# Attention and mixture of experts on one core: the stray lists emptied one by one, fewer late rows zeroed, and a new order of the steps

## Chip, cores and metric

One core of a Trainium2 chip runs the program. The metric is the device time of one execution in microseconds (us). Several executions of the kernel are timed and their median is taken; one more is profiled, and its rows are the ones shown here.

## What is computed

Attention over 8 batches with 8 heads, 576 tokens and 64 dimensions, whose keys and values are first condensed into 32 memory slots by a softmax of `phi` over the tokens, and then a top-1 mixture of 8 experts on the 4,608 tokens of 512 features that the attention gives:

```python
a = softmax(phi, axis=2)                        # 8 x 8 x 576 x 32
k_m = einsum('bhsm,bhsd->bhmd', a, k)
v_m = einsum('bhsm,bhsd->bhmd', a, v)
attn = softmax(q @ k_m.transpose(0, 1, 3, 2) / 8)
x = (attn @ v_m).transpose(0, 2, 1, 3).reshape(4608, 512)
logits = x @ w_gate                             # 512 x 8
expert_idx = argmax(logits, axis=1)
gate_w = softmax(logits)[arange(4608), expert_idx]
for e in range(8):
    mask = expert_idx == e
    h = maximum(x[mask] @ w1[e], 0)             # 512 x 1024
    out[mask] = gate_w[mask, None] * (h @ w2[e])   # 1024 x 512
```

## The kernel before

**Batches and strays.** The eight batches run one after the other, with the attention of the next batch woven into the expert work of the present one. Most tokens of a batch go to the same expert. The kernel finds that expert (step R6, `largest`; for batch 0 a guess), reads its number into SP's register (`expert_id`, L670, the TENSOR_LOAD of `ei`) and loads only its weights: w1 in four chunks of 512 KB into tiles wraw (step LW, `load_w1`, L614; batch 0 by halves, L621), w2 in four more (steps D0 to D3, `load_w2`, L631). All tokens of the batch run through this expert. Tokens that belong to another expert, the strays, are listed: GpSimd scatters one entry of 16 bytes for each token into one of five lists in DRAM, `stray_list` 0 to 4, one for each tile of 128 tokens (steps Y0 to Y4, `send_stray`, L600; a token that is no stray has a position out of bounds and writes nothing). After the last batch, `stray_slot` reads the first 32 entries (step entries, L816), gathers their attention rows from the DRAM tile `ad` (fetch, L845), runs them through their expert and scatters the rows out. The rows of strays of the last batch, which is not yet stored then, go through the DRAM tile `late` instead (L922); `fetch_late` (L730) reads rows of tiles 3 and 4 of it, and `done` (L751) adds them to that batch's output.

**What must be filled first.** A list must hold BIG wherever no entry is written, and `late` must hold zeros. The tile `empty` (128 x 336 words) is set to BIG at the start (L222). Step CE (`empty_lists`, L229 to L231) writes it into all five lists, 336 KB each. Step CY (`empty_late`, L224 to L227) clears a tile `zero`, which it takes from the pool of the output tiles (tag "y", two buffers), and writes it over all 576 rows of `late`, 1,152 KB.

**One batch.** A softmax of phi (A, A1, B, C), kvm (E, `memory`, L310: 144 small matmuls on TensorE), keys pk and values pv (G, V: L336, L347) with their copies kb and vT by ScalarE (L341, L351), scores sT (J, L441), a softmax of them and its transpose eT (K to M3), which is split into a high and a low part (S, T: eh by ScalarE, el by VectorE). A matmul of the full precision is made of three fp32r products of high and low parts. pu = V x W1 (U0, U1: L377, 16 records for each half) is split into uh by ScalarE and ul by VectorE (L381, L384). The steps i make ph (L698), 16 of them in a batch; the steps e split relu(ph) into hh and ht by ScalarE (L639) and hl, ht by VectorE (L642). The w2 chunks are split by W0 to W3: whi by ScalarE (L608), wlo by GpSimd (L609) in most batches. The steps o make py (L743, and L651 for the last, short tile), 20 parts of a batch; y0 to y4 (`done`, L756, L661, L667) scale and store the tiles (L724, 64 KB each). R to R4 make the logits, the one-hot choice and the histogram; X to X6 the gates and the positions of strays; N (L430) stores the attention rows into `ad`.

**What sets the order.** The table ORDER lists every step of the kernel once, as a batch digit and the step's name (`1LW` is LW of batch 1; `1o03` is tile 0, part 3 of its output). The program runs the steps in that order and chains the instructions of each engine in it (end of `tile_memory_attention_moe_kernel`), so each engine's queue holds them as the table lists them. SP issues nearly all DMAs, GpSimd the scatters and gathers. The DMAs of SP use eight semaphores in turn, so that a DMA also waits for the one eight places ahead of it.

```python
yp = ctx.enter_context(tc.tile_pool(name="yp", bufs=2))
late = dram.tile([S, DM], F32, name="late")
ld_list = [dram.tile([LIST, 4], F32, name="stray_list%d" % i) for i in range(NT)]
```

Of the kernel before, what the change touches and what calls it, by code (L numbers as in the profile page):

```python
# [9 lines left out]
F32 = mybir.dt.float32  # L10
# [22 lines left out]
1LW 21Q 2A2 1X4 0y3 1X 20B 21B 1T1 21C 1D0 0o12 0o13 0y1 11N 1X1 1X2 0o21 0o22 1U0 1UH10 1UH00 20Q 1UL10
1UL00 20C 0o42 0o43 0y4 0z 1D2 1D1 3LQ 0o23 0y2 1U1 1UH01 1UL01 0X2 0X5 10N 1X5 1i00 1i01 1UH11 1UL11 0X6 0Y0
2E 2D 1e01 1e00 1i03 1e03 2FV 20F 21F 1i02 1e02 1i13 1e13 2V 1i05 2G 2G1 1W0 2V1 1i17 1e17 1W1 2J 21K
20K1 1e05 2V2 1i04 1e04 20K 1W2 00N 1i06 1e06 0Y3 0Y2 1i16 1e16 1i07 1e07 21K1 3L1 21K2 20K2 20K3 21K3 1o10 1D3
1W3 3L0 21L 21M 21M0 21M1 31A 20L 2V3 20M 20M0 20M1 20M2 1i11 1e11 20M3 31Q 1i12 1e12 21M2 21M3 1o00 1o01 1o02
# [36 lines left out]
7i11 7o11 7o02 7o12 7o13 7load12 7load22 7load20 7load13 7y1 7o03 7y0 7e11 7i10 7e10 7i13 7e13 7i15 7e15 7i17 7batches 7fetch
7Y4 7attention
7o20 7rows 7o21 7rowsout 7inner 7hidden 7e17 7o22 7turn 7turned 7o23 7y2 7outer 7finish 7late4 7scatter 7Y2 7late3 7o40 7o30
7o31 7o32 7o33 7y3
7o41 7o42 7o43 7y4 7z 0i03
""".split()


# [8 lines left out]
def kernel(  # L90
# [20 lines left out]
    NT = (S + P - 1) // P  # L111
# [7 lines left out]
    LIST = E * CAP  # L119
# [12 lines left out]
    yp = ctx.enter_context(tc.tile_pool(name="yp", bufs=2))  # L132
# [39 lines left out]
    empty = const.tile([P, 1, LIST * 2 // P], F32, name="empty")  # L172
# [60 lines left out]
    def keep_warm(n, pool, tag, cols):  # L233

# [713 lines left out]
    def front(b, st, on_pool):  # L948
# [239 lines left out]
```

## Time and profile before

| What | Before |
|---|---|
| median of 3 runs | 412.94 us (411.58 to 413.81) |
| profiled execution | 411.05 us, of which the span 409.3 us |
| TensorE busy | 393.8 us, 96% of the span |
| VectorE, ScalarE, GpSimd busy | 265.9, 183.6, 180.5 us |
| DMA | 89.05 MB, mean 218 GB/s |
| TensorE's share of the chain that ended last | 83% |

The span reaches from the first to the last instruction on the chip; the 1.75 us between it and the execution's time lie around it. In the tables PE is TensorE's matmuls, PEld its weight loads, which run beside them; DVE is VectorE, ACT ScalarE, POOL GpSimd, SP the engine that issues DMAs. A busy share near 100% on one engine says that the kernel is at that engine's pace; what remains to be seen is in which places it waits. A row of a timeline gives start and length in us, the engine, the line of the kernel, the operation with its output and inputs, the count of records that follow each other, and in brackets the idle time ahead of it with what ended it.

### The profile page before, as it was taken

How to read it: one execution, taken by the hardware profiler on the slowest of the kernel's cores; microseconds unless marked ns; L12 is line 12 of the kernel's file. 1: busy time of each engine (PE TensorE's matmuls, PEld its weight loads, DVE VectorE, ACT ScalarE, POOL GpSimd, SP SyncE). 2: the span in 40 equal slices, each digit the busy share in tenths (PEclk: the TensorE clock that was granted, in tenths of full speed). 3: DMA queues.
4: the chain of work that ended last, by engine and by line, in shares of the span. 5: the costliest groups of instructions: out<-in, count | busy, mean ns of one | idle time of the engine just before them, and what ended most of it. 6: DMA issues, size and time to landing. Idle time of an engine off the chain costs nothing.

```text
span 409.3 us, 11048 instructions
## 1 busy us (share of the span) xinstructions
PE 393.8 (96%) x4221; PEld 314.8 (77%) x4221; DVE 265.9 (65%) x689; ACT 183.6 (45%) x516; POOL 180.5 (44%) x267
## 2 busy tenths in 40 slices
PE   7799999899999999999999999999999999999993
PEld 4559776588886988698878887788788878688772
DVE  6599884467854876678718858569656876672312
ACT  3168523473256625555336623584337631371210
POOL 5368611259133740255321973264452634497020
PEclk9999999999999999999999999999999999999998
DMA  8999998594194954587386926686286017469412
GB/s 263 307 376 342 331 365 275 178 373 157 56 340 140 343 200 140 222 284 265 109 284 174 367 87 208 237 273 257 74 274 233 2 28 252 110 198 317 150 42 68
DMA packets 47193, 89.05 MB, mean 218 GB/s; under 512 B 7194, under 2 KB 14622, under 8 KB 47136
## 3 DMA queue, kind: packets, MB, share of 16 engines
q1 hardware_dynamic: 43712, 83.33, 60.2%
q0 software_dynamic: 2752, 4.75, 3.2%
q8 instruction: 35, 0.57, 0.6%
q10 hardware_dynamic: 672, 0.21, 0.2%
q14 instruction: 22, 0.18, 0.1%
HBM read 71.22 MB, written 17.27 MB: 216 GB/s over the span
## 4 chain that ended last, share of the span: by engine, by line
PE 83%; DMA 5%; SPq 3%; DVE 3%; ACT 2%; issue 2%; POOL 1%; DVEq 0%; POOLq 0%; ACTq 0%
PE py L743 38%; PE ph L698 23%; PE py L651 7%; PE pu L377 4%; PE kvm L310 3%; DMA wraw<-in_moe_w_dram 3%; PE sT L441 3%; DMA kv<-in_v_dram 2%; SPq L724 1%; PE lg L484 1%; SPq L621 1%; POOL wlo L609 1%; PE pz L460 1%; PE ph L711 1%; PE spy L910 0%
## 5 line engine op out<-in xcount | busy, mean ns | idle before, releaser
L743 PE MATMUL py<-whi,hh 128*128 128x512 f32 x256 | 101.6, 397 | 0.0
L743 PE MATMUL py<-wlo,hh 128*128 128x512 f32 x256 | 100.3, 392 | 0.3 <-POOL wlo L609 0.3
L743 PE MATMUL py<-whi,hl 128*128 128x512 f32 x256 | 99.8, 390 | 0.0
L609 POOL TENSOR_TENSOR wlo<-wraw,whi 128x1024 fp32r<-128x1024 f32 x25 | 61.3, 2464 | 43.5 <-ACT whi L608 30.2
L698 PE MATMUL ph<-eh,uh 128*128 128x288 f32 x252 | 77.4, 307 | 0.0
L698 PE MATMUL ph<-eh,ul 128*128 128x288 f32 x252 | 74.4, 295 | 0.0
L642 DVE SCALAR_TENSOR_TENSOR hl<-ph,hh 128x224 fp32r<-128x224 f32 (+1 forms) x128 | 51.6, 414 | 34.9 <-ACT ht L639 21.5
L698 PE MATMUL ph<-el,uh 128*128 128x288 f32 x252 | 74.2, 294 | 0.0
L639 ACT ACTIVATE hh<-ph 128x224 fp32r<-128x224 f32 (+1 forms) x128 | 48.0, 388 | 23.6 <-PE ph L698 22.7
L743 PEld LDWEIGHTS py<-whi,hh 128*128 128x128 f32 x256 | 48.1, 188 | 11.5 <-issue 2.0
L743 PEld LDWEIGHTS py<-whi,hl 128*128 128x128 f32 x256 | 48.1, 188 | 10.4
L743 PEld LDWEIGHTS py<-wlo,hh 128*128 128x128 f32 x256 | 48.1, 188 | 9.9 <-POOL wlo L609 1.0
L600 POOL DMA_INDIRECT stray_list<-pay,posi x40 | 43.1, 1078 | 24.8 <-DMA stray_list<-pay,posi 13.1
L698 PEld LDWEIGHTS ph<-eh,uh 128*128 128x128 f32 x252 | 47.4, 188 | 5.9 <-issue 1.6
L756 ACT ACTIVATE y<-py,gw 128x512 f32<-128x512 f32 x31 | 21.2, 688 | 61.3 <-PE py L743 44.1
L698 PEld LDWEIGHTS ph<-eh,ul 128*128 128x128 f32 x252 | 47.4, 188 | 0.5
L698 PEld LDWEIGHTS ph<-el,uh 128*128 128x128 f32 x252 | 47.4, 188 | 0.0
L608 ACT CAST whi<-wraw 128x1024 fp32r<-128x1024 f32 x32 | 33.9, 1060 | 4.4 <-DMA wraw<-in_moe_w_dram 4.2
L384 DVE TENSOR_TENSOR ul<-pu,uh 128x512 fp32r<-128x512 f32 x32 | 21.0, 682 | 20.8 <-ACT uh L381 20.8
L543 POOL COPY gw<-gw 64x1 f32<-64x1 f32 x8 | 2.4, 300 | 63.8 <-DVE gw L537 63.7
L651 PE MATMUL py<-whi,ht 128*128 128x512 f32 x64 | 25.2, 394 | 0.0
L651 PE MATMUL py<-wlo,ht 128*64 128x512 f32 x64 | 24.0, 396 | 0.0
(205 smaller groups left out, 582.1 us busy)
## 6 DMA issues: line engine op xcount, KB each, us to landing
wraw<-in_moe_w_dram SPq DMA_DIRECT2D x62, 512.0 KB, 5.5
kv<-in_v_dram SPq DMA_DIRECT2D x16, 576.0 KB, 8.0
kv<-in_k_dram SPq DMA_DIRECT2D x16, 576.0 KB, 7.9
out_dram<-y SPq DMA_DIRECT2D x141, 64.0 KB, 2.7
qt<-in_q_dram SPq DMA_DIRECT2D x14, 576.0 KB, 9.5
pt<-in_phi_dram SPq DMA_DIRECT2D x15, 288.0 KB, 6.1
ad<-s_t POOLq DMA_DIRECT2D x15, 288.0 KB, 4.0
sw<-in_moe_w_dram SPq DMA_DIRECT2D x6, 512.0 KB, 6.6
```

What stands on the lines that cost most here:

```text
L310: nc.tensor.matmul(kvm[s][o0:o0 + 32, 0:2 * D], lhsT=as_[g][s0, j, c, :], rhs=kvs[g][s0, :, j, c, :], start=(c == 0), stop=(c == C - 1))
L377: nc.tensor.matmul(pu[s, n0][32 * c:32 * c + 32, :], lhsT=vT[s0, b % 2, c, :], rhs=raws[c][s0, n0:n0 + DM], start=True, stop=True)
L384: nc.vector.tensor_tensor(out=ul[:, g, n0:n0 + DM], in0=pu[g, n0], in1=uh[:, g, n0:n0 + DM].bitcast(F32), op=ALU.subtract)
L600: nc.gpsimd.indirect_dma_start(out=ld_list[i][:, :], out_offset=bass.IndirectOffsetOnAxis(ap=posi[:, i:i + 1], axis=0), in_=pay[:, i, :], ...
L608: nc.scalar.copy(out=hi, in_=raw)
L609: eng.tensor_tensor(out=lo, in0=raw, in1=hi.bitcast(F32), op=ALU.subtract)
L639: nc.scalar.activation(out=hi, in_=ph, func=AF.Relu)
L642: nc.vector.scalar_tensor_tensor(out=lo, in0=ph, scalar=0.0, in1=hi.bitcast(F32), op0=ALU.max, op1=ALU.subtract)
L651: nc.tensor.matmul(o, lhsT=l, rhs=r, start=start, stop=stop)
L698: nc.tensor.matmul(ph, lhsT=lhs[:, g, fs], rhs=rhs[:, g, s0:s1], start=(n == 0), stop=(n == 5))
L743: nc.tensor.matmul(py, lhsT=lhs[:, f, i * P:i * P + P], rhs=rhs[:, f % 2, :], start=(f == 0 and n == 0), stop=(f == KF - 1 and n == 2))
L756: nc.scalar.activation(out=y, in_=v["py", i], func=AF.Copy, scale=gate)
```

## The change

Three things.

1. **The lists are emptied one by one.** The step CE becomes CE0 to CE4, one list each. CE0 stays where CE was. CE3 and CE2, then CE4, stand among the last stores of batch 0, ahead of batch 1's D2 and D1. CE1 stands behind the stores of batch 1's tile 1, ahead of batch 2's q load.
2. **`late` is zeroed only where it is read**: rows 384 to 575, 384 KB instead of 1,152. The zeros no longer come from a tile of the pool y but from half of the rows of `empty`, which a new step CZ (`zeros`, a GpSimd memset of 64 x 256) clears in batch 3, after the last list is emptied. CY writes them in batch 6, behind 6Y2, where before it stood behind the list fills of batch 0.
3. **A new order of all steps.** The table is written anew. Most steps move by a few places on their engines; TensorE's sequence keeps nearly all of its order.

```diff
-0e10 0R1 10B 10C 11B 11C 0W0 10Q 0i15 0i11 0i12 0e12 0i14 0e14 0e15 0W1 1E 1D 10F 0e11 11F 11Q 0i13 0R2
...
+0e10 0R1 10B 10C 11B 11C 0W0 10Q 0i12 0e12 0i14 0e14 0i11 0e11 0i15 0e15 0W1 1E 1D 1FV 10F 11F 11Q 0i13
...
+    def zeros():
+        nc.gpsimd.memset(empty[0:64, :, 0:DM // 2], 0.0)
+
     def empty_late():
-        zero = yp.tile([64, 1, DM], F32, name="zero", tag="y")
-        nc.gpsimd.memset(zero, 0.0)
-        nc.sync.dma_start(out=late.rearrange("(p r) d -> p r d", p=64), in_=zero.broadcast_to([64, S // 64, DM]))
-
-    def empty_lists():
-        for t in ld_list:
-            nc.sync.dma_start(out=t.rearrange("(p h r) t -> p h (r t)", p=P, h=2), in_=empty.broadcast_to([P, 2, LIST * 2 // P]))
+        zero = empty[0:64, :, 0:DM // 2]
+        rows = late[(NT - 2) * P:S, :]
+        nc.sync.dma_start(out=rows.rearrange("(p r) (h d) -> p (r h) d", p=64, h=2), in_=zero.broadcast_to([64, (S - (NT - 2) * P) // 32, DM // 2]))
+
+    def empty_list(i):
+        nc.sync.dma_start(out=ld_list[i].rearrange("(p h r) t -> p h (r t)", p=P, h=2), in_=empty.broadcast_to([P, 2, LIST * 2 // P]))
...
-                   ("CL", constants_late), ("CE", empty_lists), ("CY", empty_late)]
+                   ("CL", constants_late), ("CZ", zeros), ("CY", empty_late)]
+            own += [("CE%d" % i, lambda i=i: empty_list(i)) for i in range(NT)]
```

The changed kernel's line numbers are 2 higher below this place.

**SP from the list fills to batch 1's w1.** Before (`wraw_1119` is the first w1 chunk of batch 1; `stray_list_91` to `95` are lists 0 to 4; the ISA rows belong to the register load and the weight addresses):

```order
L231 DMA stray_list_91<-empty 256x1x336
L231 DMA stray_list_92<-empty 256x1x336
L231 DMA stray_list_93<-empty 256x1x336
L231 DMA stray_list_94<-empty 256x1x336
L231 DMA stray_list_95<-empty 256x1x336
L243 DMA qt<-in_q_dram 128x2x576 x2
L227 DMA late<-zero 576x1x512
L724 DMA out_dram<-y 32x512 x4
L670 TENSOR_LOAD ei
L670 ISA x2
L614 ISA
L614 DMA wraw_1119<-in_moe_w_dram 128x1024
```

and now:

```order
L233 DMA stray_list_91<-empty 256x1x336
L245 DMA qt<-in_q_dram 128x2x576 x2
L726 DMA out_dram<-y 32x512 x4
L672 TENSOR_LOAD ei
L672 ISA x2
L616 ISA
L616 DMA wraw_1108<-in_moe_w_dram 128x1024
```

Four fills and the zeros are gone from this place; one fill, the q loads and the four stores remain ahead of the expert number and w1.

**SP at the w2 chunks of batch 1.** The chunks are `wraw_1224`, `wraw_1226` and, fourth, `wraw_1587` before. Before:

```order
L724 DMA out_dram<-y 32x512 x6
L631 ISA
L631 DMA wraw_1224<-in_moe_w_dram 128x2x512
L631 ISA
L631 DMA wraw_1226<-in_moe_w_dram 128x2x512
L243 DMA qt<-in_q_dram 128x2x576 x2
L724 DMA out_dram<-y 32x512 x4
L243 DMA pt<-in_phi_dram 128x2x288
L243 DMA kv<-in_k_dram 128x2x576
L243 DMA kv<-in_v_dram 128x2x576
L631 ISA
L631 DMA wraw_1587<-in_moe_w_dram 128x2x512
```

and now, where they are `wraw_1220`, `wraw_1222` and `wraw_1229` (the fill of `stray_list_94` stands directly ahead of the first row):

```order
L233 DMA stray_list_93<-empty 256x1x336
L726 DMA out_dram<-y 32x512 x2
L233 DMA stray_list_95<-empty 256x1x336
L633 ISA
L633 DMA wraw_1220<-in_moe_w_dram 128x2x512
L633 ISA
L633 DMA wraw_1222<-in_moe_w_dram 128x2x512
L245 DMA pt<-in_phi_dram 128x2x288
L245 DMA kv<-in_k_dram 128x2x576
L245 DMA kv<-in_v_dram 128x2x576
L633 ISA
L633 DMA wraw_1229<-in_moe_w_dram 128x2x512
```

Three fills stand ahead of the two chunks, two of them ahead of the last two stores; the fourth chunk and the pt and kv loads of batch 3 have moved ahead of the q loads and four stores.

**GpSimd in batch 7, between the positions of batch 6's strays and the strays' fetch.** Before:

```order
L600 DMA stray_list_92<-pay,posi 21504x4 x2
L600 DMA stray_list_94<-pay,posi 21504x4
L600 DMA stray_list_95<-pay,posi 21504x4
L600 DMA stray_list_91<-pay,posi 21504x4 x2
L430 DMA ad<-s_t 128x576
L600 DMA stray_list_92<-pay,posi 21504x4
L430 DMA ad<-s_t 128x576
L600 DMA stray_list_94<-pay,posi 21504x4
L543 COPY gz<-gz 64x1
L609 TENSOR_TENSOR wlo<-wraw_5201,whi 128x1024
L609 TENSOR_TENSOR wlo<-wraw_5299,whi 128x1024
L609 TENSOR_TENSOR wlo<-wraw_5303,whi 128x1024
```

and now:

```order
L602 DMA stray_list_94<-pay,posi 21504x4
L602 DMA stray_list_92<-pay,posi 21504x4 x2
L602 DMA stray_list_91<-pay,posi 21504x4
L602 DMA stray_list_94<-pay,posi 21504x4
L602 DMA stray_list_91<-pay,posi 21504x4
L602 DMA stray_list_92<-pay,posi 21504x4
L432 DMA ad<-s_t 128x576
L545 COPY gz<-gz 64x1
L611 TENSOR_TENSOR wlo<-wraw_5202,whi 128x1024
L611 TENSOR_TENSOR wlo<-wraw_5300,whi 128x1024
L432 DMA ad<-s_t 128x576
L611 TENSOR_TENSOR wlo<-wraw_5304,whi 128x1024
```

Here seven list entries and one DMA into `ad` stand ahead of the first wlo where there were eight and two; the other DMA into `ad` stands behind the second wlo; entries into the same list follow each other directly once instead of twice.

## Rows read from the trace of the kernel before

**Rows 1.** Busy time of each engine by stretches, with clock and DMA share

```profile
core 0: us, PE busy (x) PEld busy (x) DVE busy (x) ACT busy (x) POOL busy (x), PEclk, DMA share, GB/s
...
45.00:70.00 25.00, 25.00 (x162) 19.01 (x138) 19.15 (x49) 8.77 (x28) 8.51 (x14) 1.00 0.96 318
70.00:85.00 15.00, 12.93 (x230) 9.02 (x226) 5.98 (x15) 5.78 (x15) 5.44 (x20) 1.00 0.68 233
```

**Rows 2.** Waits of TensorE: total us, times, longest us

```profile
PE kvm L310 <- issue: 1.8, 1, 1.8
...
PE pu L377 <- DMA wraw<-in_moe_w_dram: 0.8, 2, 0.5
...
PE py L743 <- POOL wlo L609: 0.3, 1, 0.3
```

**Rows 3.** Timeline of TensorE, 66 to 84 and 168 to 171: start, length, count

```profile
68.81 1.96 PE L377 MATMUL pu<-wraw,vT 64*32 64x512 f32 x12
...
75.39 1.09 PE L377 MATMUL pu<-wraw,vT 64*32 64x512 f32 x16
...
78.19 2.23 PE L310 MATMUL kvm<-kv,pt 64*32 64x128 f32 x143
...
169.09 2.22 PE L310 MATMUL kvm<-kv,pt 64*32 64x128 f32 x144
```

**Rows 4.** Tile wraw, 62 to 72 us: what engines waited for, us, times

```profile
  DMA wraw<-in_moe_w_dram: 2.2, 3
```

**Rows 5.** Chain of waits, 40 to 84 us: start, length, what

```profile
56.33 2.23 SPq L724
...
58.61 2.39 SPq L724
...
61.53 0.30 SPq L670
...
63.98 7.02 DMA wraw<-in_moe_w_dram
```

**Rows 6.** DMA issues by kind: count, KB each, median us to landing

```profile
wraw<-in_moe_w_dram SPq DMA_DIRECT2D x62, 512.0 KB, 5.5
...
ad<-s_t POOLq DMA_DIRECT2D x15, 288.0 KB, 4.0
...
stray_list<-empty SPq DMA_DIRECT2D x5, 336.0 KB, 9.3
...
late<-zero SPq DMA_DIRECT2D x1, 1152.0 KB, 11.5
```

**Rows 7.** Timeline of ScalarE, 54 to 66 us

```profile
59.46 0.20 ACT L525 ACTIVATE ei<-es 1x1 int32<-1x1 f32 x1 [3.21 <-DVE es L523]
```

**Rows 8.** Timelines: GpSimd, ScalarE 356 to 364, GpSimd and TensorE near 100

```profile
349.15 1.18 POOL L600 DMA_INDIRECT stray_list<-pay,posi  x1 [3.68 <-DMA stray_list<-pay,posi]
...
362.51 8.11 POOL L609 TENSOR_TENSOR wlo<-wraw,whi 128x1024 fp32r<-128x1024 f32 x3
...
371.75 1.01 POOL L845 DMA_INDIRECT ag<-ad,hidx  x1 [0.99 <-POOL ag L843]
...
358.65 1.06 ACT L608 CAST whi<-wraw 128x1024 fp32r<-128x1024 f32 x1
...
98.21 2.44 POOL L609 TENSOR_TENSOR wlo<-wraw,whi 128x1024 fp32r<-128x1024 f32 x1
...
100.70 0.50 PE L743 MATMUL py<-wlo,hh 128*128 128x512 f32 x1
```

**Rows 9.** Timelines of SP, 67 to 100, and of ScalarE, 84 to 96

```profile
76.65 0.41 SPq L631 DMA_DIRECT2D wraw<-in_moe_w_dram  x1
...
87.68 0.38 SPq L631 DMA_DIRECT2D wraw<-in_moe_w_dram  x1
...
87.98 1.07 ACT L608 CAST whi<-wraw 128x1024 fp32r<-128x1024 f32 x1
...
93.53 1.05 ACT L608 CAST whi<-wraw 128x1024 fp32r<-128x1024 f32 x1 [0.98 <-DMA wraw<-in_moe_w_dram]
```

More of the change, by code (lines that the diff above doesn't have):

```diff
@@ L33 @@
[L33 to L37, printed above, removed]
@@ L74 @@
[L74 to L78, printed above, removed]
+0e10 0R1 10B 10C 11B 11C 0W0 10Q 0i12 0e12 0i14 0e14 0i11 0e11 0i15 0e15 0W1 1E 1D 1FV 10F 11F 11Q 0i13
+0e13 0R2 0R3 0o00 0i17 1G 1G1 1V 2L0 0CE0 2LQ 0X 0W3 1V1 0X1 1J 10K1 1V2 1V3 10K 10K2 10K3 21A 11K1
@@ new lines @@
+11K 11K2 0i16 0e16 10L 10M 10M0 11K3 11L 0X3 0R4 10M1 11M 11M0 11M1 11M2 0X4 10M2 10M3 1S0 0o01 0o10 0o02 0o30
+0o31 11M3 1S1 0o03 0y0 21A1 1R 1R1 1R2 1R3 0o11 0o40 20A 1X3 1R4 1R6 0e17 1T0 20A1 0o32 0o33 0o20 1LW 21Q
+2A2 0y3 1X 20B 1X4 1T1 1X1 21B 21C 1D0 0o12 0o13 11N 0y1 20Q 1X2 0o21 0o41 0o22 1U0 1UH00 1UH10 1UL10 20C
+1UL00 0o42 0o43 0y4 0CE3 0CE2 0z 0CE4 1D2 1D1 3L1 1D3 3LQ 0o23 0y2 1U1 1UH11 1UL11 1UH01 1UL01 0X2 0X5 0X6 10N
+1X5 1i00 1i01 0Y0 2E 2D 1e01 1e00 1i03 1e03 2FV 20F 21F 1i02 1e02 1i13 1e13 1i05 2G 1W0 2G1 2V 2V1 1i17
@@ new lines @@
+1e17 1W1 2J 20K1 21K 1e05 2V2 1i04 20K 1W2 00N 1i06 1e06 0Y3 1i16 1e16 1i07 1e07 21K1 20K2 21K2 21K3 1e04 20K3
+0Y2 1W3 3L0 21L 21M 21M0 31A 20L 2V3 20M 20M0 20M1 20M2 21M1 1i11 1e11 20M3 31Q 1i12 1e12 21M2 21M3 21N 1o00
+1o01 1o10 1o11 1o02 1o03 1o12 1o13 1y1 1i10 0CE1 1e10 2R 2R1 2R2 1i14 1e14 1i15 1o30 2R3 2X 2X3 2R4 2R6 2LW
+1o31 1e15 2S1 1o32 1o33 2D1 1y3 2D3 1o20 1o21 1o22 1o40 1o41 30A 2T1 30A1 31A1 3A2 30B 2X4 30C 30Q 31B 0Y4
+20N 1y0 2X2 2X1 31C 1X6 2D0 2U0 2UH00 2UL00 2S0 2T0 2X5 2X6 2UH10 3E 1o42 1o23 2W3 3D 30F 31F 2UL10 1o43
@@ new lines @@
+5L0 3D2 40C 41C 3X1 2Y2 3S1 3T1 41Q 40Q 2o41 2o42 2o43 2y4 2z 3U0 3UH10 3X2 0CZ 1Y3 3UL10 3UH00 3UL00 3W0
+3X5 4E 4D 41F 4FV 40F 3U1 3UH01 3UL01 3UH11 2o23 2y2 4G 4G1 4V 3i13 3UL11 3i15 3e15 3i02 3e13 3X6 3i03 4J
+4V1 4V2 3e02 40K 40K1 40K2 3i01 40K3 3e03 4V3 3e01 41K 3i04 3i10 3e04 3W1 50A 41K1 3i06 3e06 3i05 3e05 3e10 3i00
+3e00 41K2 3W2 2Y1 40L 40M 5LQ 50Q 3i11 3e11 3W3 40M0 40M1 3i16 3e16 3i07 3e07 41K3 41L 41M 3o00 3o01 3o02 3i14
+3e14 3o10 3o11 3o12 3o03 41M0 41M1 41M2 1Y1 41N 2Y0 40M2 40M3 50A1 41M3 5L1 51A 4R 51A1 4R1 4R2 4X 3y0 3i12
@@ new lines @@
+3i17 4R3 3e12 4S0 3o13 3y1 4X3 3e17 4R4 4R6 5A2 51B 50B 2Y4 4T0 40N 4LW 3o20 3o21 3o40 3o30 3o31 3o32 3o33
+3y3 4X1 4D0 4D2 3o41 3o42 3o43 50C 51C 3y4 4S1 51Q 3z 3o22 3o23 4U0 4UH00 4UL00 4UH10 4UL10 4D1 3y2 5E 5D
+50F 4T1 1Y4 51F 4U1 4X2 4UH01 4UL01 4i10 5G 4UH11 4UL11 4e10 5FV 5G1 4i03 4e03 4X4 4X5 4i01 4e01 4W2 4i05 4e05
+5V 4i12 5V1 4i00 4e00 5J 50K1 51K 4e12 51K1 4W1 4W0 5V2 4X6 50K 4i11 4e11 4i04 4e04 4D3 4W3 51K2 4i06 4i02
+4e02 4e06 51K3 51L 51M 51M0 50K2 4i17 4i07 4e07 50K3 50L 6LQ 6L0 1Y2 51M1 51M2 6L1 4i14 50M 50M0 4e14 60A 51M3
@@ new lines @@
+50M1 50M2 4e17 50M3 1Y0 3Y3 4Y3 51N 5V3 3Y2 50N 3Y0 3Y4 4o00 4o01 4o02 4o10 4o11 4o12 4o13 4y1 4o03 4y0 5R
+5R1 5R2 5R3 4i13 4i16 4e16 5X 61A 4e13 4o30 4o20 5X3 60A1 5R4 5R6 5LW 4i15 5D1 5D0 4o40 4o41 4e15 4o42 4o43
+61A1 5X2 6A2 5S0 60Q 60B 5X1 5T0 5S1 5T1 4Y4 61B 5X4 61C 61Q 60C 4o31 4o32 4o33 4o21 4y3 4o22 4o23 4y2
+5U0 5UH10 5UL10 5UH00 5UL00 4y4 6E 6D 60F 5X5 5X6 5Y4 4z 5U1 5UH01 5UL01 5UH11 5UL11 5i11 5i03 61F 6G 4Y2 5W1
+5e03 6G1 6FV 5i00 5e00 5e11 5W0 5i12 6V 5i02 5i01 5e01 6V1 5e12 5e02 6J 61K1 60K 60K1 5D2 5W2 6V2 5i10 5e10
@@ new lines @@
+5i14 5i04 5e14 5e04 60K2 60K3 5D3 5W3 7L0 70A 5i05 5i07 5i06 6V3 5e05 5e06 5o00 5o01 5o10 5o02 60L 5e07 60M 60M0
+7L1 7LQ 61K 61K2 61K3 70A1 61L 61M 61M0 5o03 5y0 60M1 60M2 60M3 61M1 5i16 5i15 5o11 5o12 5e15 3Y1 61M2 61N 61M3
+6R 71A 5o13 5i13 71A1 7A2 5o40 6R1 6R2 6R3 5e13 6X3 6R4 5o41 5o42 5i17 70B 6R6 5y1 70C 6X4 71B 6LW 6S1
+6T1 6X2 5e17 71C 5o30 5o31 5o32 5e16 5o33 5Y2 4Y0 6X 6X1 6X5 4Y1 5y3 5o20 5o21 5o22 6D3 6D2 6S0 6T0 70Q
+5o43 5y4 6D0 5z 5o23 5y2 6U0 6UH10 6UL10 6UH00 6UL00 6U1 6UH11 6UH01 6UL01 7E 7D 70F 6X6 7FV 6UL11 6i10 6e10 71Q
@@ new lines @@
+60N 6W3 71F 6i00 6i13 6e13 6i12 7V 7G 6i03 6i02 6i05 7V1 6e00 6e12 6W2 7G1 7V2 6W0 6e03 6e02 7J 70K1 70K
+70K2 70K3 6Y2 0CY 6D1 5Y0 6W1 6i14 6e14 6i01 6e05 6e01 71K1 71K 6i16 6i11 6e11 70L 6i15 6e15 7V3 6e16 6i06 71K2
+6e06 70M 6i07 6e07 70M0 70M1 70M2 6i04 6i17 6o00 6o01 6e04 6o02 6o03 71K3 6o10 70M3 71L 71M 71M0 71M1 71M2 71M3 6Y4
+5Y3 7S0 7T0 7R 7R1 7R2 7R3 6o30 7X3 7R4 6y0 7S1 7X 7R6 7T1 7X1 6e17 7X4 7X2 7X5 7LW 7X6 6Y3 5Y1
+6Y1 6Y0 7Y3 7Y0 7Y1 71N 7table 7D0 6o20 6o21 6o22 6o23 6o11 6o12 6o13 6y1 6y2 6o40 6o31 7U0 7UH10 7UL10 7UH00 7UL00
@@ new lines @@
+6o41 6o42 6o43 6y4 7D1 7D2 7D3 7entries 7load11 6z 7load21 6o32 6o33 6y3 7load10 7i02 7e02 7U1 7UH01 7UL01 7UH11 7UL11 7i03
+7e03
+7X7 7W0 7i01 7i06 7e01 7e06 7W1 70N 7i16 7e16 7i12 7e12 7i04 7e04 7i07 7e07 7i11 7i00 7i05 7e00 7i14 7o00 7o01 7o10
+7W2 7e05 7o02 7W3 7gather 7e14 7o11 7o12 7o13 7load12 7load20 7load13 7load23 7o03 7y1 7load22 7e11 7i10 7e10 7y0 7i13 7e13
+7i15 7e15
+7i17 7batches 7fetch 7Y4 7attention 7o20 7rows 7rowsout 7o21 7inner 7hidden 7e17 7o22 7turn 7turned 7o23 7y2 7outer 7finish
@@ L79 @@
+7late3 7late4 7scatter 7Y2 7o40
+7o30 7o31 7o32 7o33 7y3 7o41 7o42 7o43 7y4 0i03 7z
 """.split()
```

50 lines of the change are left out of this document (8 added, 42 removed).

## Prediction

> **What bounds the kernel now.** I read the busy time by stretches first. TensorE (PE) is busy without a gap from 45 to 70 us and lacks 2.07 us in the 15 us from 70 to 85 [rows 1]. Its granted clock is 1.00 while it works, the upper of its two levels, so no part of this argument is about the clock. The page gives it 96% of the span. TensorE is the bound: a new order can only win what TensorE loses to waits, and the next question is where those are.
>
> The table of TensorE's waits names only small ones: 1.8 us once in front of a kvm matmul, released by "issue" (nothing that the profile shows), 0.8 us in front of pu for a weight chunk, 0.3 us in front of py for a wlo tile [rows 2]. It understates one place. A pu stage of 16 records stands in the timeline at 75.39 us with 1.09 us; the first one of batch 1, at 68.81, needs 1.96 us for its first 12 records alone [rows 3]. Asked for the tile wraw in that stretch, the trace puts 2.2 us of waiting, in three pieces, down to the landing of weight chunks [rows 4]; most of it lies in the weight loads, so that TensorE still looks busy. **This is the largest recoverable loss of the kernel.**
>
> Why the chunks are late stands in the chain of waits: two output stores of batch 0 hold SP's queue for 2.23 and 2.39 us, at 56.33 and 58.61, the expert number is loaded at 61.53, and the fourth w1 chunk, issued at 63.98, needs 7.02 us to land, at 71.00 [rows 5]. The DMA engines are 96% busy with 318 GB/s from 45 to 70 us [rows 1], and the five list fills of 336 KB, which take 9.3 us to land, and the 1,152 KB of zeros for `late`, which take 11.5, are in that traffic [rows 6]. The stores stand behind it because the program gives SP's DMAs eight semaphores in turn: each waits until the one eight places ahead has landed.
>
> **The change part by part.** Fills and zeros: four of the five fills and all of `late` leave this place, 4 x 336 + 1,152 = 2,496 KB, at 318 GB/s 8 us of transfer ahead of w1. The two long stores then cost an issue of 0.41 us [rows 9] like others and end 2.23 + 2.39 - 0.82 = 3.8 us sooner. Another wait comes last instead, ScalarE's ei, which now runs from 59.46 to 59.66 behind VectorE's es [rows 7]. The change puts both ahead of the hl and ht of one step, so ei is done some 0.4 us sooner, at about 59.3 (estimated as the two short VectorE rows that no longer stand ahead of it). SP then loads the number at 59.4 instead of 61.53, 2.1 us sooner, and issues the fourth chunk at 61.9. It lands 5.5 us later, the median of such a load [rows 6], or at worst the 7.02 measured here: 67.4 to 68.9. TensorE asks for the first chunk at 68.81 and, at 1.09 us for 16 records, for the fourth at 69.6. **The whole 2.2 us goes.** Ends: 0 if the issue does not move, -2.2. I take -2.2, since even the slowest landing measured here is in time.
>
> The wait for wlo in batch 7: GpSimd (POOL) starts the first of three wlo tiles at 362.51, although ScalarE began the cast that it needs at 358.65 and took 1.06 us; until then GpSimd posts list entries, and one that follows another into the same list waits 3.68 us for it to land [rows 8]. The new order has two DMAs fewer ahead of the first wlo and one such pair in place of two, some 3.7 us less, so GpSimd is ready with the cast even though the cast comes sooner with TensorE. The 0.3 us wait [rows 2] goes: -0.3, ends 0 and -0.3.
>
> The 1.8 us in front of kvm: I take 0. The stage at 169.09 does its 144 matmuls in 2.22 us; the one at 78.19 does 143 in 2.23 and then waits 1.8 us for the last [rows 2, 3]. In the new order the same number of TensorE instructions stands ahead of it, nearly all in the same sequence, so what is tied to its place in the stream stays. Ends: 0 and -1.8. The Trainium skill, "Runtime: NRT & Kernel Launch", section "Instruction fetch mechanics", says that instructions are refilled in blocks of 256 and that crossing a block's edge is mostly hidden; by that rule the gap is no refill and could go with the traffic, which is rival (1) below. The one gap of 1.8 us neither proves nor refutes it.
>
> What is added: CE3, CE2 and CE4 (336 KB each) now stand among the last stores of batch 0, ahead of the w2 chunks of batch 1, which SP issued from 76.65 and whose first cast ran at 87.98 [rows 9]. 5.5 us after its issue a chunk has landed, at 82.2: 5.8 us to spare. CE3 and CE2 go out while SP waits for the last rows of batch 0 anyway; CE4 costs an issue, 0.4, and 336 KB at 318 GB/s, 1.1 us. 1.5 of 5.8; both ends of this slack follow TensorE, so it is not shortened by the 2.2 us. 0, upper end +1. CE1 and the 384 KB of CY go out later, where the page's DMA row has slices far below full; CZ is one short memset while GpSimd waits for other work: 0 each.
>
> What could take the gain back at once is the last wlo of batch 1. GpSimd makes it from 98.21 for 2.44 us, and TensorE uses it at 100.70 [rows 8]: just in time, and now wanted 2.2 us sooner. GpSimd's run to it goes by ScalarE's casts, which follow TensorE. Its own cast, at 93.53, waited 0.98 us for the fourth w2 chunk, which SP issued at 87.68 [rows 9]; 2.2 us sooner, the cast is still in time if it starts by 98.21 - 2.2 - 1.05 = 94.96. The change moves this chunk (1D3) ahead of the qt loads and four stores, though behind pt and two kv loads. Even issued no sooner than now it is there at 93.5. 0; upper end +2.2, all of the gain, if GpSimd does not move with TensorE. The other exchanges (V with G, hl with el) lie on engines that are not the bound, where TensorE does not wait; the stores at the end stay. 0, ends -0.3 and +0.5.
>
> **Sum:** -2.2 - 0.3 = -2.5 us. The profiled execution took 411.05 us and would take 408.5. The median of the runs shown is 412.94, 1.9 above it; I apply the difference to the median: 410.4.
>
> **Rivals.** (1) The gap before kvm goes as well, because it hangs on the traffic rather than on the place in the stream: -4.3, so 408.6. For it: the stage at 169.09 has no gap. Against it: three fills and the kv loads now come close ahead of it. 0.10. (2) The gain is given back: w1 lands in time, but a tile that is ready just in time now, like the last wlo of batch 1 or one of a later batch, is not ready 2.2 us sooner. It keeps 0 to 1 us of 2.5: 412.4. For it: GpSimd's posts wait for each other's landing, and there it does not follow TensorE. 0.25. (3) The change does not do what it says: the stores stay blocked by the kv loads in flight, and w1 is issued no sooner. Only the 0.3 is left: 412.6. 0.04. (4) Slower, in batch 7: the change puts the post of `ad` (70N) behind the second wlo, and the fetch of the strays reads `ad`. If GpSimd's first wlo starts no sooner than 362.51, two wlo of 8.11 / 3 us end at 367.9, `ad` is posted and lands 4.0 us later, at 371.9 to 372.5, and the fetch, at 371.75 now [rows 6, 8], runs up to 0.7 us later than now; the wait for wlo takes the 2.2 back on the way, and the fetch's delay falls on the stray steps that TensorE does last: +0.7, 413.6. It decides from a start of the first wlo at 361.8 on. Against it: the new order has fewer posts there. 0.06.
>
> **How the numbers follow.** My forecast has 0.55; with its ends it reaches from 409.6 to 411.2. About what a measurement of this kernel can tell from no change is 0.5%, 2.06 us: below 410.88 is faster. Faster: 0.45 of the forecast's 0.55 and all of (1), 0.55. Slower: (4) alone stays within the bound, but two such waits together, or one of them with the +1 of the w2 chunks, pass it: 0.05. Same: the rest, 0.40. The range takes in the forecast, (2), (3) and nearly half of (1): 408.3 to 412.9.
>
> **What would show it.** Right: pu of batch 1 at about 1.1 us for 16 records and no wait for wraw; the stores ahead of w1 at about 0.4 us; ei as the last thing before w1; still 1.8 us in front of kvm; no wait for wlo in batch 7. Wrong: pu still waiting; a new wait of py for wlo in any batch. Below 409 the kvm gap has gone, or the later batches held more than the rows show.

## The result and the profile after

The changed kernel takes 407.85 us (median of 7 runs, 407.28 to 409.24), the kernel before 412.48 (7 runs, 410.25 to 413.81). The ratio is 0.9898, with a 95% interval of 0.9871 to 0.9926: faster by 4.6 us, 1.0%. The prediction was 410.4 with a range from 408.3 to 412.9; the sign is right, the size is not, and the time lies 0.45 us below the range. The forecast started from 412.94, the median of three executions of the kernel before; with the seven here that median is 412.48, so 0.46 us of the miss lie in where the forecast started. The profiled execution took 407.33 us with a span of 405.6, against 411.05 and 409.3 before.

Where the time went is seen at the starts of the same stages in the two timelines of TensorE:

| Stage, start in us | before | after | difference |
|---|---|---|---|
| pu of batch 1, first half | 68.81 | 68.34 | -0.47 |
| pu of batch 1, second half | 75.39 | 73.42 | -1.97 |
| kvm of batch 2 | 78.19 | 76.22 | -1.97 |
| sT of batch 2 | 86.95 | 83.08 | -3.87 |
| lg (router logits) of batch 2 | 105.58 | 102.78 | -2.80 |
| pu of batch 7, second half | 356.11 | 353.24 | -2.87 |
| last matmul | 402.05 | 398.54 | -3.51 |
| end of the span | 409.3 | 405.6 | -3.7 |

So there are five steps on TensorE: -0.5 at the start, -1.5 in pu of batch 1, **-1.9 at kvm**, **+1.1 between sT and lg**, -0.6 in batch 7. (The kvm that the prediction discusses is that of batch 2, which runs inside batch 1's expert work.) From 103 to 353 us the difference stays within 0.15 us: 250 us of new order that win and lose nothing.

The busy time by stretches answers to [rows 1]:

```profile
core 0: us, PE busy (x) PEld busy (x) DVE busy (x) ACT busy (x) POOL busy (x), PEclk, DMA share, GB/s
45.00:70.00 25.00, 25.00 (x142) 18.93 (x142) 19.20 (x48) 8.70 (x27) 7.63 (x13) 1.00 0.71 242
70.00:85.00 15.00, 15.00 (x310) 11.96 (x309) 8.88 (x22) 9.57 (x25) 5.75 (x21) 1.00 0.84 291
85.00:120.00 35.00, 34.03 (x298) 27.70 (x302) 24.85 (x62) 13.85 (x41) 17.00 (x24) 1.00 0.67 241
```

From 45 to 70 us the DMA engines are now 71% busy with 242 GB/s instead of 96% and 318. The 2.07 us that TensorE lost from 70 to 85 are gone; in the next stretch it has a new loss of 0.97. The table of its waits answers to [rows 2]; columns as there:

```profile
PE pu L379 <- DMA wraw<-in_moe_w_dram: 1.1, 2, 0.8
PE py L745 <- DVE hl L644: 1.0, 1, 1.0
```

The wait before kvm and the one for wlo are no longer in it; a wait of py for hl is new. The tile wraw from 60 to 72 us, for [rows 4]:

```profile
  DMA wraw<-in_moe_w_dram: 0.6, 1
```

And the timeline of TensorE for [rows 3]:

```profile
68.34 1.77 PE L379 MATMUL pu<-wraw,vT 64*32 64x512 f32 x16
...
73.42 1.09 PE L379 MATMUL pu<-wraw,vT 64*32 64x512 f32 x16
...
76.22 2.29 PE L312 MATMUL kvm<-kv,pt 64*32 64x128 f32 x143
...
78.35 0.27 PE L312 MATMUL kvm<-kv,pt 64*32 64x128 f32 x1
```

The first half of pu takes 1.77 us for all 16 records, where its first 12 took 1.96; the second half takes 1.09 as before. kvm's last row follows the 143 others without a gap. The weight loads of pu's first half show where its last wait is, in front of the fourth chunk:

```profile
68.34 0.17 PEld L379 LDWEIGHTS pu<-wraw,vT 64*32 64x32 f32 x12 [0.35 <-issue]
69.07 0.14 PEld L379 LDWEIGHTS pu<-wraw,vT 64*32 64x32 f32 x4 [0.56 <-DMA wraw<-in_moe_w_dram]
```

SP's queue, for [rows 5] and [rows 9]:

```profile
55.58 2.31 SPq L726 DMA_DIRECT2D out_dram<-y  x4
59.80 2.12 SPq L616 DMA_DIRECT2D wraw<-in_moe_w_dram  x4
...
74.72 0.54 SPq L233 DMA_DIRECT2D stray_list<-empty  x1
75.50 1.72 SPq L633 DMA_DIRECT2D wraw<-in_moe_w_dram  x2
```

The four stores ahead of w1 are issued in 2.31 us; before, two of them alone took 4.62. The first chunk of w1 goes out at 59.80 instead of 62.32, and the expert number is ready sooner (ScalarE, for [rows 7]):

```profile
58.79 0.20 ACT L527 ACTIVATE ei<-es 1x1 int32<-1x1 f32 x1 [3.24 <-DVE es L525]
```

### The profile page after: what moved, and what is told of

Same layout as the page of the kernel before. It is cut to its first block, busy times and chain, and to the rows that moved or that the text cites. A ratio compares the mean times of both kernels' runs of the same rounds, so it can differ in the third digit from the quotient of the medians.

```text
span 405.6 us, 11054 instructions
## 1 busy us (share of the span) xinstructions
PE 392.5 (97%) x4221; PEld 314.5 (78%) x4221; DVE 264.9 (65%) x689; ACT 183.3 (45%) x516; POOL 178.1 (44%) x267
## 4 chain that ended last, share of the span: by engine, by line
PE 93%; DVE 2%; DMA 2%; SPq 1%; issue 1%; ACT 0%; DVEq 0%; ACTq 0%
PE py L745 43%; PE ph L700 25%; PE py L653 7%; PE pu L379 4%; PE kvm L312 4%; PE sT L443 3%; PE pw L241 2%; DMA wraw<-in_moe_w_dram 2%; PE lg L486 1%; SPq L623 1%; DVE s_t L407 1%; PE pz L462 1%; PE spy L912 0%; PE sph L892 0%; PE ph L713 0%
## 5 line engine op out<-in xcount | busy, mean ns | idle before, releaser
L611 POOL TENSOR_TENSOR wlo<-wraw,whi 128x1024 fp32r<-128x1024 f32 x25 | 60.3, 2424 | 29.9 <-ACT whi L610 28.3
L602 POOL DMA_INDIRECT stray_list<-pay,posi x40 | 42.2, 1056 | 21.7 <-issue 7.7
```

Of the source, the lines that this page charges most:

```text
L602: nc.gpsimd.indirect_dma_start(out=ld_list[i][:, :], out_offset=bass.IndirectOffsetOnAxis(ap=posi[:, i:i + 1], axis=0), in_=pay[:, i, :], ...
L611: eng.tensor_tensor(out=lo, in0=raw, in1=hi.bitcast(F32), op=ALU.subtract)
```

## The experiments

Two theories to begin with. **L**: the fills and zeros that were moved carry the gain, and the 1.8 us in front of kvm went because of the loads around it. **O**: the new order carries it. For the gap itself: **T**, TensorE's next instructions arrive late behind bulk loads; **S**, it belongs to a place in the instruction stream; **D**, it is a late datum. Line numbers differ by a few between these kernels, since the table of the order is written in more or fewer lines.

### The fills and zeros alone

```diff
-0CE
+0CE0
...
-0y4 0z 1D2 1D1
+0y4 0CE3 0CE2 0z 0CE4 1D2 1D1
...
+0CE1
...
+0CZ
...
+0CY
```

(0CE1 behind 1y1, 0CZ behind 3X2, 0CY behind 6Y2, the old 0CY gone, and the three functions of the change.)

> The kernel before with the first two parts of the change alone: fills CE0 to CE4 one by one and the smaller zeros of late, at the places in the old order that answer to the new ones; every other step in the old order. Theory L (the fills and zeros carry the gain): pu of batch 1 waits under 1 us for wraw instead of 2.2, the 1.8 us gap in front of kvm of batch 1 is gone too, because it hangs on the loads around it, and the time is 3 to 4 us below before, near 409. Rival O (the new order carries it): 0 to 1 us below before, near 412.

Measured: ratio 0.9879 to the kernel before (0.9824 to 0.9933), median 409.32 against 413.88 on that chip. Theory L holds for this part and O falls: this part alone does what the whole change does. The wait for wraw, and kvm:

```profile
  DMA wraw<-in_moe_w_dram: 0.3, 1
```

```profile
77.68 2.28 PE L308 MATMUL kvm<-kv,pt 64*32 64x128 f32 x144
```

Between the two halves of pu 1.8 us are won, at kvm 2.0, and no wait for hl appears. In this one profiled execution pu of batch 1 begins 1.25 us later than before, which hides that much of the gain in its span of 407.8. The trace shows why: TensorE waited 2.0 us for a w1 chunk of batch 0, and behind that wait the granted clock was 0.50, the lower of its two levels (1.2 instead of 2.4 GHz), from 23.1 to 26.5 us; the 16 records of pu there took 3.61 us.

```profile
23.06 3.61 PE L375 MATMUL pu<-wraw,vT 64*32 64x512 f32 x16 [2.04 <-DMA wraw<-in_moe_w_dram]
```

### The new order alone

```diff
-0CE0
+0CE
...
-10K3 21A
+10K3 0CY 21A
...
-0y4 0CE3 0CE2 0z 0CE4 1D2 1D1
+0y4 0z 1D2 1D1
```

(0CE1, 0CZ and the later 0CY are left out likewise, and the three functions are those of before.)

> The new order alone: all five lists and all of late are filled where they were before. Theory L: pu of batch 1 still waits about 2 us, the gap in front of kvm is still about 1.8 us, and the time is within 1.2 us of before, near 411.8. Rival O: 3 us or more below before, near 409.

Measured: ratio 0.9952 (0.9914 to 0.9989), 411.72 against 413.88: 2.2 us won, more than the 1.2 that theory L allowed, less than the 3 of O. pu waits nearly as before:

```profile
  DMA wraw<-in_moe_w_dram: 1.9, 3
```

The forecast for the gap missed: kvm takes 2.59 us and 1.6 us of the gap are gone with the fills where they were.

```profile
78.04 2.59 PE L306 MATMUL kvm<-kv,pt 64*32 64x128 f32 x143
```

In the new order SP issues two w2 chunks at 76.67 but no q loads behind them (3LQ has moved). So two parts of the change each take most of the gap away, and their gains must not be added. The wait of py for hl is here too (0.98 us at 95.70), so it comes with the new order and not with the fills.

### Loads moved behind kvm

```diff
-0z 1D2 1D1 3LQ 0o23 0y2
+0z 0o23 0y2 1D2 1D1 3LQ
```

> The kernel before with three steps moved on SP alone: 1D2, 1D1 and 3LQ stand behind the stores of 0y2, so that these loads go out near 81.8 us, after kvm, instead of 76.65 to 78.7, just ahead of it. Theory T (the gap is the next instructions of TensorE arriving late behind bulk loads): the gap is under 0.3 us, kvm takes about 2.2 us for 144 matmuls; the time is 1 to 2 us below before, less what w2 may be late. Rival S (the gap belongs to a place in the instruction stream, whatever the traffic): still 1.8 us, and the time as before or up to 1 us above.

Measured: ratio 0.9958 (0.9926 to 0.9991). The gap row is left with 0.19 us, all TensorE rows of kvm and ahead of it in the same order as before:

```profile
78.01 2.23 PE L306 MATMUL kvm<-kv,pt 64*32 64x128 f32 x143
80.44 0.27 PE L306 MATMUL kvm<-kv,pt 64*32 64x128 f32 x1 [0.19 <-issue]
```

S alone falls, T holds: nothing was changed but the time of these loads on SP. From sT to lg 0.65 us are given back: TensorE, now sooner, waits 0.56 us for the last wlo of batch 1, which GpSimd starts at 97.09, as soon as a list entry and a subtraction ahead of it are done. This is the loss that the prediction feared in its rival (2).

### The instruction stream shifted by 64 rows

```diff
+def tiny(n):
+    pt_ = ps_mm.tile([P, 4, 16], F32, name="pw", tag="mm")
+    for _ in range(n):
+        nc.tensor.matmul(pt_[0:32, 0, :], lhsT=ones[0:64, 0:32], rhs=ones[0:64, 0:16], start=True, stop=True)
...
                     keep_warm(*args)
+                    if args[-1] == 256:
+                        tiny(16)
```

> The kernel before with 16 very small matmuls more in batch 0, in a wait of TensorE near 16 us; they shift everything behind them by 64 rows of the instruction stream, and nothing else moves. Their results are not used. Theories T and S, by both of which the place in the stream has a part: the gap in front of the last kvm matmul of batch 1 goes or moves, and the time is 1 to 2 us below before. Rival D (the gap is a late datum or a semaphore of the loads, and has nothing to do with the instruction stream): still 1.8 us at the same matmul, and the time as before.

Measured: **slower**, ratio 1.0062 (1.0028 to 1.0097), where faster was expected. (The sixteen matmuls are 32 records of TensorE, each with its weight load.) The gap in front of kvm's last matmul is gone, as T and S said and D did not. But others came that no kernel had before:

```profile
17.33 1.03 PE L245 MATMUL pw<-ones 64*32 64x16 f32 x16 [1.69 <-issue]
...
44.07 0.40 PE L703 MATMUL ph<-eh,uh 128*128 128x288 f32 x1 [1.42 <-issue]
...
89.80 0.72 PE L446 MATMUL sT<-qT,kb 32*32 32x288 f32 x18 [0.47 <-issue]
...
127.87 0.50 PE L656 MATMUL py<-whi,ht 128*128 128x512 f32 x1 [1.07 <-issue]
...
175.73 1.04 PE L382 MATMUL pu<-wraw,vT 64*32 64x512 f32 x3 [0.52 <-issue]
```

Counted in rows of TensorE's stream (a weight load, a matmul and a semaphore wait are a row each), these five stand at 1.76, 4.76, 8.75, 11.76 and 15.75 times 256; the gap before stands at 7.75 times 256. All six lie at three quarters of a block of 256, in or just behind a stage that ran through its rows fast (kvm runs 288 rows in 2 us, py 256 rows in 29).

The traces also hold the packets of the instruction queue, 16 KB each: in the kernel before, 31 of them come while TensorE passes 7,880 rows, 254 rows for each. In all six gaps the next row of TensorE starts 1.2 to 1.5 us after the end of the packet that belongs to that place (by their order), and TensorE had come to the place at most 0.3 us after the packet's end, or ahead of it. At the other places of this kind in the two traces the packet had ended more than 1.2 us earlier, and there is no such gap. So these gaps are late instructions. A sixth new gap, 0.42 us in front of pa at 387.06, lies at 31.28 times 256 and is not one of them; what it is was not tried.

The new gaps outweigh the one that went, 5.2 us against 1.8, but they are not the whole of the slowdown. In the profiled execution the granted clock was 0.50 from 17.4 to 24.2 us, behind the first of the new gaps, where the kernel before had 1.00, and TensorE waited 2.31 us for eh at 28.08, which it does not in the kernel before (columns as in the busy time by stretches):

```profile
17.40:24.10 6.70, 6.31 (x101) 3.69 (x102) 3.30 (x8) 1.06 (x4) 0.64 (x1) 0.50 0.92 318
```

Of the ten executions, the two with a mean granted clock of 0.995 or more took 414.1 and 414.3 us, the other eight, at 0.992 or less, 415.8 to 418.7. The ten executions of the kernel before with 0.995 or more have a median of 412.7. By these few the gaps alone cost some 1.5 us (an estimate), and the rest of the 2.7 goes with the clock; whether the gaps bring the clock down was not tried.

### The traffic put back

The changed kernel with the q loads ahead of kvm again:

```diff
-0z 0CE4 1D2 1D1 3L1 1D3 3LQ 0o23 0y2
+0z 3LQ 0CE4 1D2 1D1 3L1 1D3 0o23 0y2
```

> The changed kernel with the two q loads of batch 3 (1,152 KB) moved ahead of the last fill and of the w2 chunks of batch 1, so that they go out near 74.7 us, 1.5 us ahead of kvm, as such loads did in the kernel before. Theory T (the gap is TensorE's next instructions arriving late behind bulk loads): the gap in front of the last kvm matmul is back with 1 to 2.5 us. Rival C (the gap went because of the changed order on TensorE or the earlier time of kvm): it stays under 0.3 us.

Measured (one profiled execution, 408.35): the gap is back, 1.84 us, in the new order and with the fills in their new places. SP issued the q loads at 73.41:

```profile
73.41 0.96 SPq L241 DMA_DIRECT2D qt<-in_q_dram  x2
```

```profile
74.91 2.22 PE L308 MATMUL kvm<-kv,pt 64*32 64x128 f32 x141
78.97 0.30 PE L308 MATMUL kvm<-kv,pt 64*32 64x128 f32 x2 [1.84 <-issue]
```

With this T stands from both sides for this gap. The packet of the instruction queue that lands around this kvm ends 2.66 us after kvm's start in the kernel before and 2.82 with the traffic put back, and the gaps between two kvm matmuls there are 2.07 and 2.11 us. It ends 0.63 us after it in the changed kernel and 0.73 in the fills-alone kernel, with 0.05 and 0.02 at that place. The kernels between lie between: 1.48 with 0.84 us (the subtractions apart, below), 1.16 with 0.46 (loads moved), 1.07 with 0.34 (order alone).

### The wait for hl

First the order on VectorE:

```diff
-21K3 1e04 20K3 0Y2
+1e04 21K3 20K3 0Y2
```

> The changed kernel with one step moved: 1e04 (hh and hl of one step of batch 1) stands ahead of 21K3 and 20K3, two subtractions of the next batch's softmax, instead of between them. Theory H (TensorE's new wait of 1.0 us for hl near 93.6 us comes from the order on VectorE alone): the wait is gone and everything behind it runs 0.9 to 1.0 us sooner. Rival W (TensorE then waits for the last wlo of batch 1, which GpSimd makes in the same stretch): py waits about as long for wlo instead, and nothing is gained.

Measured (one profiled execution, 407.43): the wait for hl is gone and no wait for wlo takes its place. From sT to lg 1.25 us are won. But kvm, 0.3 us sooner, has 0.5 us of its gap again (longest step 0.81 us), so that the stages behind lg run 0.7 to 1.0 us sooner, and in batch 7 TensorE waits 0.87 us for ohr where it waited 0.43: the end is as it was.

Why hl was late is in the rows of the changed kernel, VectorE, GpSimd and TensorE near 91 us:

```profile
90.89 2.25 DVE L407 TENSOR_TENSOR s_t<-s_t,mm 128x576 f32<-128x576 f32 x1
93.07 0.45 DVE L644 SCALAR_TENSOR_TENSOR hl<-ph,hh 128x288 fp32r<-128x288 f32 x1
...
90.30 1.03 POOL L602 DMA_INDIRECT stray_list<-pay,posi  x1 [0.30 <-DMA out_dram<-y]
91.33 1.19 POOL L407 TENSOR_TENSOR s_t<-s_t,mm 128x576 f32<-128x576 f32 x1
...
93.57 0.50 PE L745 MATMUL py<-whi,hh 128*128 128x512 f32 x1 [0.97 <-DVE hl L644]
```

VectorE's subtraction of 128 x 576 takes 2.25 us where the five others of the same line take 0.75 to 0.99, and GpSimd's, of the same form, falls within it. The test moves only GpSimd's:

```diff
-21K3 1e04 20K3 0Y2 1W3
+21K3 1e04 0Y2 20K3 1W3
```

> The changed kernel with GpSimd's subtraction 20K3 moved behind the list entry 0Y2, as it stood before, so that it no longer runs at the same time as VectorE's subtraction 21K3. Theory B (the two block each other): VectorE's subtraction near 91 us, which takes 2.25 us in the changed kernel, takes 0.75 to 0.8, hl follows 1.4 us sooner and TensorE's wait for hl is gone or under 0.2 us. Rival: it is slow for another reason (list entries, its data) and takes 2 us or more again.

Measured (one profiled execution, 407.05):

```profile
91.05 0.76 DVE L403 TENSOR_TENSOR s_t<-s_t,mm 128x576 f32<-128x576 f32 x1
...
90.47 1.03 POOL L598 DMA_INDIRECT stray_list<-pay,posi  x1 [0.30 <-issue]
91.80 0.99 POOL L598 DMA_INDIRECT stray_list<-pay,posi  x1 [0.31 <-DVE s_t L403]
92.81 1.18 POOL L403 TENSOR_TENSOR s_t<-s_t,mm 128x576 f32<-128x576 f32 x1
```

0.76 us, with a list entry beside it as before (90.47) but no GpSimd subtraction, and TensorE's wait for hl is gone. So it is the two subtractions, not the entries. The kernel before has the like at 100.39 us (a VectorE product of 128 x 576 that takes 2.00 us, with GpSimd's of the same line at 100.57 within it) and in batch 7 (VectorE's wlo 3.08 us instead of 1.22, beside GpSimd's); there TensorE was not waiting for it. The Trainium skill, "SBUF — State Buffer", section "Who interferes with whom", says that a VectorE instruction with two SBUF inputs contends with a GpSimd instruction that reads SBUF; these rows agree.

### More work ahead of pu

The run on hl, and with it:

```diff
-1U0 1UH00 1UH10 1UL10 20C 1UL00 0o42
+0o42 1U0 1UH00 1UH10 1UL10 20C 1UL00
```

> As the run before, and 0o42 stands ahead of 1U0, so that TensorE has about 1 us more of batch 0's work to do before it needs w1 of batch 1, for which it still waits 0.6 us in the changed kernel. Expected if both waits are only a matter of order: 1.5 us below the changed kernel's 407.85, near 406.4, a ratio of 0.985 to before. Rival: the waits come back one step later (pu or ph of batch 1, wlo), and the time is that of the changed kernel within 0.5 us.

Measured: ratio 0.9887 (0.9865 to 0.9908), median 408.20: nothing beyond the changed kernel, as the rival had it. The first half of pu no longer waits for w1, but from the second half to kvm it takes 0.9 us more than in the changed kernel, and kvm has 0.8 us of its gap. That half takes 1.98 us for its 16 records instead of 1.09; the trace puts 0.8 us, in its weight loads, down to ScalarE's y of batch 0 (L754), so a wait came back one step later, as the rival said.

### A better version

Three moves from these findings, on the changed kernel: GpSimd's 20K3 behind 0Y2; the last fill CE4 behind the stores of 0y2, away from kvm; and 6o31 ahead of 7X3, where TensorE waits 0.4 to 0.9 us for ohr.

```diff
-0z 0CE4 1D2 1D1 3L1 1D3 3LQ 0o23 0y2
+0z 1D2 1D1 3L1 1D3 3LQ 0o23 0y2 0CE4
...
-20K3 0Y2
+0Y2 20K3
```

> The changed kernel with two moves: GpSimd's 20K3 behind the list entry 0Y2 (no overlap of the two subtractions), and the last fill CE4 behind the stores of 0y2, so that 336 KB less are under way just ahead of kvm of batch 1. By theories B and T: VectorE's subtraction near 91 us takes 0.76 us, TensorE has no wait for hl, the gap in front of the last kvm matmul stays under 0.5 us, and the time is 1 us below the changed kernel of the same call. Rival: kvm, now a little sooner, still meets the w2 loads and has a gap near 0.8 us, as with the first of these moves alone; then 0.3 us below the changed kernel.

```diff
-6o30 7X3
+6o30 6o31 7X3
...
-6o40 6o31 7U0
+6o40 7U0
```

> As the run before, and 6o31 stands ahead of 7X3, so that TensorE has 1.4 us of work instead of a wait of 0.6 to 0.9 us for ohr near 333 us. Expected: that wait is gone and 0.5 us more are won, if w1 of batch 7, which is asked for 0.8 us later, still lands before its pu near 345. Rival: pu of batch 7 waits for wraw instead, and nothing is won.

> The changed kernel once more, unaltered, to stand beside the two runs before on the same chip. Expected: a ratio of 0.988 to 0.991 to the kernel before, no gap in front of kvm of batch 1 above 0.5 us, and 0.9 to 1.0 us of waiting for hl near 93.6 us.

Measured side by side, each against the kernel before: the changed kernel again 0.9894 (0.9860 to 0.9928), median 408.78, with 1.0 us of waiting for hl and 0.38 us as kvm's longest step; the first two moves 0.9876 (0.9843 to 0.9909), 408.12, where 1 us below the changed kernel was expected; all three **0.9835 (0.9794 to 0.9875), 406.06**. The first two moves are in the trace as expected (subtraction 0.76 us, no wait for hl, kvm's longest step 0.35 us) but are worth 0.7 us in the medians, which these runs cannot tell from nothing. With all three the wait for ohr is gone too, and pu of batch 7 does not wait for wraw:

```profile
70.00:85.00 15.00, 15.00 (x309) 11.85 (x308) 9.04 (x23) 9.52 (x25) 5.92 (x21) 1.00 0.86 304
85.00:120.00 35.00, 35.00 (x348) 28.70 (x347) 24.50 (x67) 14.10 (x43) 16.55 (x24) 1.00 0.71 246
320.00:360.00 40.00, 40.00 (x240) 31.79 (x240) 28.46 (x75) 15.87 (x42) 22.06 (x29) 1.00 0.41 133
360.00:380.00 20.00, 20.00 (x228) 17.29 (x227) 8.21 (x28) 5.89 (x16) 9.34 (x9) 1.00 0.82 272
```

TensorE is busy in all of these 110 us. Some waiting hides in weight loads, though: the first half of pu of batch 7 takes 1.65 us instead of 1.09, and the trace puts the difference down to ScalarE's y. The third move was expected to be worth 0.5 us; the medians say 2.1, which that wait does not explain, and the profiled executions with two and with three moves have the same span, 404.8 us. This kernel has the lowest median of all; its interval still overlaps that of the changed kernel, so that the gain of the third move is not shown.

## Why the prediction was wrong

- **The step that failed is "The 1.8 us in front of kvm: I take 0."** Its premise was that the gap is tied to its place in the stream, and the place stayed. It did stay (7.75 times 256 rows in both), and the gap went all the same. The runs put a product in place of an either-or: it needs a fast stage ahead of a block's edge *and* a fetch that comes late, here behind bulk loads. Shifting the place removes it there (64 rows), so does moving the loads (behind kvm, or by the new order), and putting the loads back brings it back. Whether loads had a part in the five gaps of the shifted stream was not tried. Measured: -1.9 (-1.5 in a second profile of the changed kernel). This term alone moves the sum from -2.5 to -4.4. The other misses (+0.7 in pu, +1.1 for hl, -0.3 more in batch 7, -0.5 at the start and -0.2 behind the last matmul) come to +0.7 before rounding, which gives the -3.7 of the two spans; the medians say -4.6, with 3.1 to 5.3 for the interval.
- Rival (1) named the right mechanism with 0.10. What spoke against it, "three fills and the kv loads now come close ahead of it", was judged by their bytes and not by when SP issues them. Two fills went out at 69.86, well ahead, the third at 74.72, 1.1 us ahead of the packet's start and without harm, and the kv loads at 78.88, behind the fetch; the 1,152 KB of q loads, which had gone out just ahead of the fetch, had moved to 80.50. The section on the change names that move; the prediction used it for 1D3 only.
- The Trainium skill, "Runtime: NRT & Kernel Launch", section "Instruction fetch mechanics", says that instructions come in blocks of 256 and that a crossing is mostly hidden. The first agrees with six gaps at the same place in a block. The second holds for 31 of the 32 such places in the kernel before, several of them in kvm stages; the one left cost 2.1 us. The prediction used the second half as a reason to doubt that the gap was a fetch; it was one.
- *pu of batch 1, -2.2*: right in kind, 1.5 of it came, 1.8 in the fills-alone kernel. The stores, the number and the issue moved as worked out (fourth chunk out at about 61.6 against 61.9 forecast). Two readings were off. The worst landing was not 7.02 us: the fourth chunk, issued at 61.59, held TensorE until 69.07, 7.5 us later. And TensorE does not ask for the fourth chunk 0.8 us behind the first: the weight loads for the first three chunks all start within 0.06 us, at 68.34 to 68.40, so that the fourth was wanted at about 68.4. That leaves 0.6 us of waiting.
- *wlo of batch 7, -0.3*: right. GpSimd starts it at 357.43, 5.1 us sooner, and TensorE does not wait. Behind it the fetch of the strays does wait for `ad` as rival (4) had it, 1.48 us, but at 368.52, 3.2 us sooner than before, and nobody waits for it:

```profile
357.43 4.76 POOL L611 TENSOR_TENSOR wlo<-wraw,whi 128x1024 fp32r<-128x1024 f32 x2
362.14 0.59 POOL L432 DMA_DIRECT2D ad<-s_t  x1
364.50 2.39 POOL L611 TENSOR_TENSOR wlo<-wraw,whi 128x1024 fp32r<-128x1024 f32 x1 [1.78 <-ACT whi L610]
366.84 0.20 POOL L845 MEMSET ag<- 64x128 f32 x1
368.52 1.01 POOL L847 DMA_INDIRECT ag<-ad,hidx  x1 [1.48 <-DMA ad<-s_t]
```

- *The other exchanges, 0, ends -0.3 and +0.5*: wrong in size. "Lie on engines that are not the bound" is no argument where the engine that bounds takes their result next: TensorE waited 0.97 us for hl, and 1.07 us were lost there. No row of before could show the overlap of that pair, but the row at 100.39 of that trace, which the prediction does not show, has the price of such an overlap, and the order shows which steps come to stand side by side.
- *w2 behind the fills, and the last wlo of batch 1, 0*: right; TensorE waits for neither.
- *The start*: the span gained 0.5 us there without a reason in the change. Over the profiled runs pu of batch 1 begins from 1.15 us sooner to 1.25 us later than the one it is compared with, among kernels that do the same work up to it (the one with 64 rows more left out). In the kernel with the fills alone it was a late w1 chunk of batch 0 and a stretch at the lower granted clock; for the others the cause was not tried. One kernel differs by as much from profile to profile: the changed one begins pu at 68.34 in one and 67.66 in another.

## What to carry to other kernels

Wait tables name what an engine waited for only when a semaphore says so; a gap with no releaser, in or behind a run of very short matmuls, should be set against the instruction queue's packets, against the stream position in blocks of 256 rows and against what the DMA queues were given in the 3 us before it (the loads that mattered here went out 1 to 3 us ahead of the packet's start), and can be tested by moving a load that nobody needs yet. When bulk fills are moved, list by issue time, and not only by bytes, what stands ahead of the next such stage. When steps are reordered, look for VectorE and GpSimd instructions with two inputs that come to overlap, and ask whether the engine that bounds takes the next result of either. Before a slowdown is put down to one cause, compare the granted clock of the executions.

## What the runs showed that was not expected

- A kernel with sixteen small matmuls more was 2.7 us slower (ratio 1.0062): five gaps of 0.47 to 1.69 us appear at three quarters of a block of 256 rows, to which they shifted the rest of the stream, and eight of its ten executions had a mean granted clock of 0.992 or less, against seven of 25 of the kernel before.
- A fill of 336 KB lands in 3.7 us (median) where fills go out in ones and twos, against 9.3 in the row of five [rows 6]; a w1 or w2 chunk in 4.9 instead of 5.5:

```profile
wraw<-in_moe_w_dram SPq DMA_DIRECT2D x62, 512.0 KB, 4.9
...
stray_list<-empty SPq DMA_DIRECT2D x5, 336.0 KB, 3.7
```

- Two subtractions of 128 x 576 on VectorE and GpSimd at once took 2.25 us for VectorE's, three times its 0.76 alone.
